# An attention turn of two score tiles and a whole PV step in place of three tiles and half steps

## The chip, the cores and the metric

The kernel runs on one core of one Trainium2 chip. The metric is device time in microseconds of one execution, the median of several runs. The core's engines are TensorE (PE in the profile, with its weight loads as PEld), VectorE (DVE), ScalarE (ACT), GpSimd (POOL) and SyncE (SP, which here issues DMAs).

## The reference

Two independent layers share a sequence of 2048 rows of 512 channels, and their outputs are laid side by side:

```python
q = (x @ wq).reshape(B, S, 32, 16).transpose(0, 2, 1, 3)   # 32 heads of 16
k = x @ wk                                                 # one key and value head
v = x @ wv
p = softmax(einsum("bhqd,bkd->bhqk", q, k) * 16 ** -0.5)
a = (p @ v).transpose(0, 2, 1, 3).reshape(B, S, 512) @ wo

k_shift = causal depthwise convolution of B_k, 4 taps
kv = k_shift * B_v
b = B_q * (long causal convolution of kv along S (by FFT) + kv * ssm_D)
out = concatenate([a, b], -1)
```

## The kernel before, in words

**Attention.** The 32 heads times 2048 queries are cut into 32 blocks (`NQ`) of 2048 rows: four heads with 512 queries each. For each block the kernel walks over the 16 key tiles of 128 (`NKT`), 512 steps in all. A step has two score tiles `s` of 128 keys by two heads of 512 queries (`scores`, L770 to L793): two fp16 matmuls of 512 columns at L784, on two row tiles of the array, and one exponential of 1024 columns on ACT at L792 that writes an fp32 tile `p`. `s` has three buffers of two PSUM banks each, `p` has seven. PV (`pv`, L795) multiplies `p` with the values, extended by a column of ones for the softmax's denominator, in fp32: four matmuls on four column tiles of the array, one for each head, that sum over the 16 key tiles in one PSUM bank `acc`. Here PV goes by half steps: at L821 each of the four matmuls has 256 columns, first the left half of a step, then the right. After 16 steps DVE copies the bank to `ao` (L831), SP sends it to DRAM (L833), and the next block takes the other bank of the pool `pf`, or the same one again.

The last block (`n == NQ - 1`) is cut by queries instead, in two halves of 256 columns (L806), so that the first half's result `al` (L815) is there early.

**The turn.** `attend` (L837) writes the order of the work by hand. A turn emits three score tiles (L841 to L844) and then the PV of up to three half steps. Three tiles of a turn fill all three buffers of `s`.

**Fill.** All else runs in the gaps: six generators (L1213) for the query projections, the convolution's transforms, its element-wise work on DVE, the output projection and so on. Each yields the cost of its next piece, in units for PE (four matmuls: 512 fp16 columns, or 128 fp32 columns) and nanoseconds for DVE, and `_Fill.step` (L1049) lets it go on when credit is left. `turn` (L1045) adds `RATE` to the credit once a turn, up to `MOST`. A generator that is neither the convolution's nor in a hurry gets at most `EASY` units a turn (L1065). `attend` calls `step` ahead of PV for a piece that continues an open PSUM bank, and behind PV for new ones (L857, L863); where a turn changes the PV bank (`full`, L854), the new ones come right ahead of the first PV of the new bank instead. Fill and PV share the two banks of `pf`: with `acc` in one, all fill groups pass through the other, and each has to be copied out by DVE before the next begins. Matmuls of the fill are at L203 (`mm`), transposes at L305, the bound at L638.

**The end.** In the last turn `fill.finish()` (L849) runs what is left of the fill; then come the PV of the last tiles and `last` (L988), which normalizes the second half of the last block on DVE (`over`, L975: six instructions with two 32x32 transposes), multiplies with the last rows of `wo` (`wl`), and adds the sums `wp` of all earlier heads. For row blocks 0 and 2 of the output `wp` is put into PSUM by a matmul with the identity and ACT copies the result; for 1 and 3 DVE adds it.

Of the kernel before, what the change touches and what calls it, by code (L numbers as in the profile page):

```python
# [8 lines left out]
F32 = mybir.dt.float32  # L9
# [5 lines left out]
ALU = mybir.AluOpType  # L15
# [4 lines left out]
P = 128  # L20
S = 2048
D = 512
H = 32
DH = 16
NKT = S // P
NQ = 4 * H // 4
# [19 lines left out]

RATE = 3.0, 2500.0
EASY = 2  # L50
MOST = 4.0, 2900.0
WO_AT = 240, 345, 430
OB = 5

# [36 lines left out]
WAIT = -1.0  # L91
# [4 lines left out]
class _Emit:  # L96
# [695 lines left out]
        self.nc.scalar.activation(p, s, AF.Exp, scale=DH**-0.5 / SC / SC)  # L792
        self.pt[u] = p  # L793

    def pv(self, x):  # L795


        nc, w = self.nc, self.w
        i, h = x // 2, x % 2
        n, k = i // NKT, i % NKT  # L800
        if n == NQ - 1:
            h, k = divmod(x % (2 * NKT), NKT)
            if k == 0:
                self.acc = self.bank()
            for j in range(4):
                nc.tensor.matmul(  # L806
                    self.acc[32 * j : 32 * j + 32, 0:256],
                    self.vx[:, k, :],
                    self.pt[x][:, j % 2, 256 * (j // 2) : 256 * (j // 2) + 256],
                    start=k == 0,  # L810
                    stop=k == NKT - 1,
                )
            if k == NKT - 1 and h == 0:
                self.al = w.tile([P, 512], F32, tag="r", bufs=1, name="al")
                nc.vector.tensor_copy(self.al[:, 0:256], self.acc[:, 0:256])  # L815
            return
        if k == h == 0:
            self.acc = self.bank()
        cols = slice(256 * h, 256 * h + 256)
        for j in range(4):  # L820
            nc.tensor.matmul(  # L821
                self.acc[32 * j : 32 * j + 32, cols],
                self.vx[:, k, :],
                self.pt[2 * i + j // 2][:, j % 2, cols],
                start=k == h == 0,
                stop=k == NKT - 1 and h == 1,
            )
        if k < NKT - 1 or h == 0:
            return
        a = w.tile([P, 512], F32, tag="ao", bufs=1, name=self.nm("ao"))  # L830
        nc.vector.tensor_copy(a, self.acc)  # L831
        if n < NQ - 2:
            nc.sync.dma_start(self.od[n], a)  # L833
        else:
            self.ao = a

    def attend(self, fill):  # L837
        self.od = self.dr.tile([NQ, P, 512], F32, name="od")
        x, steps = 0, NQ * NKT
        for u in range(3, 2 * steps + 3, 3):  # L840
            for t in range(u, min(u + 3, 2 * steps)):  # L841
                if t % 32 == 12 and 2 <= t // 32 + 1 < NQ:
                    self.stack(t // 32 + 1)
                self.scores(t)  # L844
            self.step = x // 2

            end = 2 * (min(u, 2 * steps) // 2) if u >= 2 * steps else min(x + 3, 2 * (u // 2))
            if u >= 2 * steps:
                fill.finish()  # L849
                self.lb = [self.wide()[:, 0, :] for _ in range(2)]  # L850
                self.mm(self.lb[0], self.ident, self.wp[0], stop=False)


            full = [y for y in range(x + 1, end) if y % (2 * NKT) == 0 or y == (2 * NQ - 1) * NKT]  # L854
            fill.turn()
            if not full:
                fill.step(self.step, False)  # L857
            for y in range(x, end):
                if y in full:
                    fill.step(self.step, True)  # L860
                self.pv(y)
            if not full:
                fill.step(self.step, True)  # L863
            x = end
        self.last()


    def heads(self, G):
# [53 lines left out]
    def wo_row(self, b, i, G, last):  # L922
        pairs = self.three(self.oc[G][:, :, i * P : (i + 1) * P], self.wo[G % 4])
        yield from self.products(b, pairs, last, 700 * last)

    def wo_part(self):
        nc, w, I = self.nc, self.w, self.I
        xr = self.out.rearrange("b (c p i) d -> (b c) p i d", c=4, p=P, i=4)
        for c in range(3):
            yield from self.after(("oc", 4 * c + 3))  # L930
            for i in range(4):
                b = yield from self.wo_rows(i, range(4 * c, 4 * c + 4))
                t = self.s2("wp", (512,))
                nc.vector.tensor_scalar(t, b, 1 / (OS * WS), None, ALU.mult)  # L934
                nc.sync.dma_start(xr[c][:, i, 0:D], t)
            self.seen.update(("wo", G) for G in range(4 * c, 4 * c + 4))

        yield from self.after(("oc", 13), f"q{3}")
        self.wp = [w.tile([P, D], F32, tag="wq", bufs=4, name=self.nm("wp")) for _ in range(4)]
        for i in range(4):  # L940
            b = yield from self.wo_rows(i, range(12, 14))
            nc.vector.tensor_scalar(self.wp[i], b, 1 / (OS * WS), None, ALU.mult)

        self.wl = []
        for q in range(2):
            t = w.tile([P, D], F32, tag="xt", bufs=2, name=self.nm("wl"))
            nc.gpsimd.memset(t, 0.0)
            for j in range(4):
                h = H - 8 + 4 * q + j
                nc.sync.dma_start(t[32 * j : 32 * j + DH, :], I["A_wo"][DH * h : DH * h + DH, :])  # L950
            self.wl.append(t)
        yield from self.after(("oc", 14))
        for i in range(4):
            b = []
            yield from self.wo_row(b, i, 14, True)
            nc.vector.scalar_tensor_tensor(self.wp[i], b[0], 1 / (OS * WS), self.wp[i], ALU.mult, ALU.add)
        both = w.tile([P, 2, 4, 512], F32, tag="in", bufs=1, name="lr")
        t, self.lr = both[:, 0], both[:, 1]
        while self.step < NKT * (NQ - 1) + 1:
            yield WAIT, 1  # L960
        for h in range(2):
            yield 0, 1800
            self.over(self.ao[:, 256 * h : 256 * h + 256], t, h)
        for i in range(4):
            if i == 2:

                while self.step < NKT * (NQ - 1) + NKT // 2 + 1:
                    yield WAIT, 1
                yield 0, 1800
                self.over(self.al[:, 0:256], self.lr, 0)  # L970
            b = []
            yield from self.columns(b, 0, t[:, 2, i * P : (i + 1) * P], self.wl[0], True, 700)
            nc.vector.tensor_tensor(self.wp[i], self.wp[i], b[0], ALU.add)

    def over(self, a, t, h):  # L975


        v = self.nc.vector
        r, s, o = (t[:, i, h * 256 : (h + 1) * 256] for i in range(3))
        v.transpose(r, a)  # L980
        col = r.rearrange("p (b c) -> p b c", c=32)[:, :, DH : DH + 1]
        v.tensor_scalar(col, col, 1e-30, None, ALU.max)
        v.reciprocal(col, col)
        v.tensor_copy(s.rearrange("p (b c) -> p b c", c=32), col.broadcast_to([P, 8, 32]))
        v.transpose(r, s)
        v.tensor_tensor(o, a, r, ALU.mult)

    def last(self):  # L988

        nc = self.nc  # L990
        xr = self.out.rearrange("b (c p i) d -> (b c) p i d", c=4, p=P, i=4)
        t = self.w.tile([P, 2, 4, 512], F32, tag="big", bufs=2, name="lb")[:, 0]
        s = self.lb + [self.wide()[:, 0, :], self.bank()]
        y = [self.s2("y", (512,)) for _ in range(4)]
        rows = lambda x, i: x[:, 2, i % 2 * P : (i % 2 + 1) * P]
        for i in range(2):
            self.mm(s[i], rows(self.lr, i), self.wl[1], start=i > 0)
        nc.scalar.copy(y[0], s[0])
        self.mm(s[2], self.ident, self.wp[2], stop=False)
        self.over(self.acc[:, 0:256], t, 0)  # L1000
        for i in range(2, 4):
            self.mm(s[i], rows(t, i), self.wl[1], start=i > 2)
        nc.vector.tensor_tensor(y[1], self.wp[1], s[1], ALU.add)
        nc.scalar.copy(y[2], s[2])
        nc.vector.tensor_tensor(y[3], self.wp[3], s[3], ALU.add)
        for i in range(4):
            (nc.scalar, nc.sync)[i % 2].dma_start(xr[3][:, i, 0:D], y[i])


class _Fill:  # L1010
# [34 lines left out]
    def turn(self):  # L1045
        self.used = 0
        self.credit = [min(c + r, m) for c, r, m in zip(self.credit, RATE, MOST)]

# [191 lines left out]
```

## Time and profile before

| | |
|---|---|
| time, median of 3 runs | 1048.03 us (1046.55 to 1048.33) |
| span of the profiled execution | 1043.5 us |
| median less span | 4.5 us |
| PE busy | 990.4 us (95%) |
| ACT busy | 972.4 us (93%) |
| DVE busy | 654.4 us (63%) |
| mean granted TensorE clock | 0.996 |

The span runs from the first to the last instruction of one profiled execution; the time of a run holds in addition what lies around that, so the two are 4.5 us apart here. In the views quoted below a row begins with its start in microseconds from the span's start, then its length, the engine, the source line, the operation, the tile written and the tiles read, and the number of instructions merged into the row; in square brackets stands the engine's idle time before it and what ended that. An fp32 matmul of the program shows as two records, so PV of three half steps, twelve matmuls, is x24.

### The profile page before, as it was taken

The page shows a single profiled execution, that of the slowest core. Times are in us where ns is not written, and L with a number is a line of the kernel's source. Part 1 is how long each engine was busy: PE and PEld are TensorE (multiplying, and loading weights), DVE is VectorE, ACT ScalarE, POOL GpSimd, SP SyncE. Part 2 cuts the span into 40 slices and gives each one's busy share as a digit, 9 for nine tenths or more (in the row PEclk, how much of TensorE's full clock was granted, in tenths as well). Part 3 has the DMA queues.
Part 4 walks back from the last instruction along what each step waited for, and adds up shares of the span by engine and source line. Part 5 has one row for each costly group of instructions (what it writes and reads, how often), then busy time and mean ns, then how long its engine had stood idle before and what let it go on. Part 6 is the DMA issues. An engine that isn't in the chain of part 4 may idle for free.

```text
span 1043.5 us, 31945 instructions
## 1 busy us (share of the span) xinstructions
PE 990.4 (95%) x14019; PEld 449.3 (43%) x14019; DVE 654.4 (63%) x881; ACT 972.4 (93%) x1039; POOL 105.0 (10%) x158
## 2 busy tenths in 40 slices
PE   6899999999999999999999999999999899999986
PEld 4344444444433334444444444444444334444432
DVE  4736873877497887776861578378888990211133
ACT  4699989999999999999999999999999999999994
POOL 4131301000000000030101312000000000121000
PEclk9999999999999999999999999999999999999999
DMA  7335524112211211031314534101032101331101
GB/s 243 128 97 181 190 77 167 45 51 82 91 56 45 75 35 40 22 122 57 96 56 132 183 123 149 42 20 44 33 97 71 52 29 40 109 121 45 51 2 44
DMA packets 47549, 87.30 MB, mean 84 GB/s; under 512 B 11132, under 2 KB 26026, under 8 KB 46380
## 3 DMA queue, kind: packets, MB, share of 16 engines
q1 hardware_dynamic: 33996, 43.50, 12.9%
q0 software_dynamic: 11648, 40.89, 12.1%
q8 instruction: 111, 1.82, 0.7%
q10 hardware_dynamic: 1760, 0.81, 0.3%
q14 instruction: 34, 0.28, 0.1%
HBM read 60.16 MB, written 25.02 MB: 82 GB/s over the span
## 4 chain that ended last, share of the span: by engine, by line
PE 70%; ACT 15%; DVE 8%; issue 6%; DMA 1%; ACTq 0%; SPq 0%
PE f L821 32%; PE s L784 22%; ACT p L792 14%; PE f L203 14%; DVE sp L141 2%; DVE ao L831 1%; PE f L305 1%; PE f L806 1%; DMA wqf<-in_A_wq 1%; DVE xT L540 1%; PE x L203 0%; ACT xT L539 0%; DVE sp L395 0%; DVE sp L255 0%; DVE t L362 0%
## 5 line engine op out<-in xcount | busy, mean ns | idle before, releaser
L792 ACT ACTIVATE p<-s 128x1024 f32<-128x1024 f32 x1024 | 960.1, 1037 | 41.5 <-PE s L784 35.9
L821 PE MATMUL f<-p,vx 128*32 128x256 f32 x7936 | 494.7, 381 | 8.1 <-DVE ao L831 8.1
L784 PE MATMUL s<-st,kst 49*128 49x512 f16 x2048 | 317.6, 380 | 19.1 <-ACT p L792 16.4
L821 PEld LDWEIGHTS f<-p,vx 128*32 128x32 f32 x7936 | 235.1, 110 | 196.9 <-issue 33.6
L784 PEld LDWEIGHTS <-kst 49*128 49x128 f16 x2048 | 100.1, 94 | 253.3 <-issue 206.5
L141 DVE TENSOR_TENSOR sp<-sp 128x1024 f32<-128x1024 f32 x96 | 111.5, 1213 | 0.0
L255 DVE COPY sp<-f 128x512 f32<-128x512 f32 x64 | 44.1, 689 | 63.6 <-PE f L203 62.5
L831 DVE COPY ao<-f 128x512 f32<-128x512 f32 x31 | 21.4, 691 | 71.4 <-PE f L821 71.4
L203 PE MATMUL f<-xT,wq 128*32 128x512 f16 x768 | 58.8, 391 | 0.1
L141 DVE TENSOR_TENSOR sp<-sp,sp 128x1024 f32<-128x1024 f32 x48 | 56.3, 1216 | 0.2
L203 PE MATMUL f<-wo,o 128*32 128x512 f16 x720 | 54.4, 383 | 0.0
L426 DVE TENSOR_TENSOR r<-f,q 128x512 f32<-128x512 f32 x16 | 11.0, 688 | 63.0 <-PE f L203 63.0
L259 POOL DMA_DIRECT2D ff<-in_ff x32 | 17.5, 548 | 266.7 <-PE f L203 266.7
L203 PE MATMUL f<-a,ff 128*32 128x256 f32 (+1 forms) x648 | 38.8, 338 | 1.6 <-DVE sp L255 1.6
L203 PE MATMUL f<-hT,ff 128*32 128x256 f32 (+1 forms) x648 | 38.8, 338 | 0.0
L203 PE MATMUL f<-sp,fi 128*32 128x256 f32 (+1 forms) x680 | 38.3, 331 | 0.0
L427 POOL DMA_DIRECT2D out<-r x16 | 11.5, 717 | 250.1 <-DVE rl L879 147.0
L364 DVE TENSOR_TENSOR a<-a,t 128x512 f32<-128x512 f32 x48 | 33.2, 691 | 1.5
L362 DVE TENSOR_TENSOR t<-kk,tpb 128x512 f32<-128x512 f32 x48 | 32.7, 681 | 0.0
L934 DVE TENSOR_SCALAR wp<-f 128x512 f32<-128x512 f32 x12 | 8.3, 690 | 38.8 <-PE f L203 38.8
L619 DVE TENSOR_SCALAR cut<-f 128x512 f32<-128x512 f32 x16 | 11.0, 689 | 32.3 <-PE f L203 32.2
L203 PEld LDWEIGHTS f<-a,ff 128*32 128x32 f32 x648 | 18.0, 109 | 17.2 <-issue 6.3
(141 smaller groups left out, 602.6 us busy)
## 6 DMA issues: line engine op xcount, KB each, us to landing
ff<-in_ff POOLq DMA_DIRECT2D x32, 256.0 KB, 5.0
od<-ao SPq DMA_DIRECT2D x30, 256.0 KB
kk<-in_B_k POOLq DMA_DIRECT2D x12, 640.0 KB, 4.9
qd<-qp SPq DMA_DIRECT2D x48, 128.0 KB
st<-qd SPq DMA_DIRECT2D x60, 98.0 KB
v<-in_B_v POOLq DMA_DIRECT2D x16, 256.0 KB, 4.8
hin<-in_B_ssm_k POOLq DMA_DIRECT2D x4, 1024.0 KB, 6.8
fi<-in_fi POOLq DMA_DIRECT2D x16, 256.0 KB, 3.8
```

The lines of the kernel that those rows point to most:

```text
L141: v.tensor_tensor(part(out), part(a), part(b), op)
L203: self.nc.tensor.matmul(out[j : j + 32], w[:, j : j + 32], x, start=start, stop=stop)
L255: self.nc.vector.tensor_copy(c[:, :, m, :], b[0].rearrange("p (q n) -> p q n", q=2))
L259: self.nc.gpsimd.dma_start(t, self.I[n][:, 2 * m2 : 2 * m2 + 2])
L362: nc.vector.tensor_tensor(t, kx(i), tap(i), ALU.mult)
L364: nc.vector.tensor_tensor(a, a, t, ALU.add)
L426: nc.vector.tensor_tensor(r, b[0].rearrange("p (i n) -> p i n", i=2), q[m2], ALU.mult)
L427: nc.gpsimd.dma_start(self.orr[:, 2 * m2 : 2 * m2 + 2, D + blk * CB : D + (blk + 1) * CB], r)
L784: self.nc.tensor.matmul(s[:, e, :], self.kst[rows, k * P : (k + 1) * P], part(rows), start=True, stop=True,)
L792: self.nc.scalar.activation(p, s, AF.Exp, scale=DH**-0.5 / SC / SC)
L821: nc.tensor.matmul(self.acc[32 * j : 32 * j + 32, cols], self.vx[:, k, :], self.pt[2 * i + j // 2][:, j % 2, cols], start=k == h == 0, sto ...
L831: nc.vector.tensor_copy(a, self.acc)
```

## The change

A turn of `attend` now emits two score tiles and then one whole step of PV: four matmuls of 512 columns (in the last block, two half steps as before). The bank of PV changes only between turns; there the fill's new pieces come ahead of PV. The credits are given per turn of two tiles: 1.8 units and 1700 ns, where a turn of three had 3.0 and 2500. `EASY` stays at 2 a turn.

At the end, the leftover fill runs before the PV of the last two tiles; the product for block 0 stands between these two, that for block 1 behind the second. DVE adds `wp` for blocks 0, 1 and 3, behind the normalization; ACT copies block 2 alone. SP's queue sends blocks 0 and 1, ACT's queue 2 and 3. In `wo_part`, the normalization of the first half of the last block moves behind the four products with `wl[0]`.

```diff
-RATE = 3.0, 2500.0
+RATE = 1.8, 1700.0
 EASY = 2
-MOST = 4.0, 2900.0
+MOST = 3.0, 2900.0
...
-    def pv(self, x):
+    def pv(self, i):
...
-        if k == h == 0:
+        if k == 0:
             self.acc = self.bank()
-        cols = slice(256 * h, 256 * h + 256)
         for j in range(4):
             nc.tensor.matmul(
-                self.acc[32 * j : 32 * j + 32, cols],
+                self.acc[32 * j : 32 * j + 32, :],
                 self.vx[:, k, :],
-                self.pt[2 * i + j // 2][:, j % 2, cols],
-                start=k == h == 0,
-                stop=k == NKT - 1 and h == 1,
+                self.pt[2 * i + j // 2][:, j % 2, :],
+                start=k == 0,
+                stop=k == NKT - 1,
             )
...
     def attend(self, fill):
         self.od = self.dr.tile([NQ, P, 512], F32, name="od")
-        x, steps = 0, NQ * NKT
-        for u in range(3, 2 * steps + 3, 3):
-            for t in range(u, min(u + 3, 2 * steps)):
+        steps = NQ * NKT
+        for i in range(steps - 1):
+            for t in range(2 * i + 3, min(2 * i + 5, 2 * steps)):
                 if t % 32 == 12 and 2 <= t // 32 + 1 < NQ:
                     self.stack(t // 32 + 1)
                 self.scores(t)
-            self.step = x // 2
...
+            self.step = i
             fill.turn()
-            if not full:
+            if i % NKT == 0 or i == (2 * NQ - 1) * NKT // 2:
+                fill.step(self.step, True)
+                self.pv(i)
+            else:
                 fill.step(self.step, False)
-            for y in range(x, end):
-                if y in full:
-                    fill.step(self.step, True)
-                self.pv(y)
-            if not full:
+                self.pv(i)
                 fill.step(self.step, True)
-            x = end
-        self.last()
+        self.last(fill)
...
-    def last(self):
+    def last(self, fill):
...
+        fill.finish()
         t = self.w.tile([P, 2, 4, 512], F32, tag="big", bufs=2, name="lb")[:, 0]
-        s = self.lb + [self.wide()[:, 0, :], self.bank()]
+        self.pv_last(4 * NQ * NKT // 2 - 2)
+        s = [self.wide()[:, 0, :]]
...
-        for i in range(2):
-            self.mm(s[i], rows(self.lr, i), self.wl[1], start=i > 0)
-        nc.scalar.copy(y[0], s[0])
+        self.mm(s[0], rows(self.lr, 0), self.wl[1])
+        self.pv_last(4 * NQ * NKT // 2 - 1)
+        self.over(self.acc[:, 0:256], t, 0)
+        s += [self.wide()[:, 0, :], self.wide()[:, 0, :], self.bank()]
+        self.mm(s[1], rows(self.lr, 1), self.wl[1])
         self.mm(s[2], self.ident, self.wp[2], stop=False)
-        self.over(self.acc[:, 0:256], t, 0)
         for i in range(2, 4):
             self.mm(s[i], rows(t, i), self.wl[1], start=i > 2)
-        nc.vector.tensor_tensor(y[1], self.wp[1], s[1], ALU.add)
+        for i in range(2):
+            nc.vector.tensor_tensor(y[i], self.wp[i], s[i], ALU.add)
         nc.scalar.copy(y[2], s[2])
         nc.vector.tensor_tensor(y[3], self.wp[3], s[3], ALU.add)
         for i in range(4):
-            (nc.scalar, nc.sync)[i % 2].dma_start(xr[3][:, i, 0:D], y[i])
+            (nc.sync, nc.scalar)[i // 2 % 2].dma_start(xr[3][:, i, 0:D], y[i])
```

More of the change, by code (lines that the diff above doesn't have):

```diff
@@ L793, in scores @@
         self.pt[u] = p
-    def pv(self, x):
+    def pv(self, i):
         nc, w = self.nc, self.w
-        i, h = x // 2, x % 2
         n, k = i // NKT, i % NKT
         if n == NQ - 1:
[L802 to L815, printed above, removed]
+            for x in (2 * i, 2 * i + 1):
+                self.pv_last(x)
             return
-        if k == h == 0:
+        if k == 0:
             self.acc = self.bank()
-        cols = slice(256 * h, 256 * h + 256)
         for j in range(4):
             nc.tensor.matmul(
-                self.acc[32 * j : 32 * j + 32, cols],
+                self.acc[32 * j : 32 * j + 32, :],
                 self.vx[:, k, :],
-                self.pt[2 * i + j // 2][:, j % 2, cols],
-                start=k == h == 0,
-                stop=k == NKT - 1 and h == 1,
+                self.pt[2 * i + j // 2][:, j % 2, :],
+                start=k == 0,
+                stop=k == NKT - 1,
             )
-        if k < NKT - 1 or h == 0:
+        if k < NKT - 1:
             return
@@ L835, in pv, with pv_last @@
             self.ao = a
+    def pv_last(self, x):
+        nc, w = self.nc, self.w
+        h, k = divmod(x % (2 * NKT), NKT)
+        if k == 0:
+            self.acc = self.bank()
+        for j in range(4):
+            nc.tensor.matmul(
+                self.acc[32 * j : 32 * j + 32, 0:256],
+                self.vx[:, k, :],
+                self.pt[x][:, j % 2, 256 * (j // 2) : 256 * (j // 2) + 256],
+                start=k == 0,
+                stop=k == NKT - 1,
+            )
+        if k == NKT - 1 and h == 0:
+            self.al = w.tile([P, 512], F32, tag="r", bufs=1, name="al")
+            nc.vector.tensor_copy(self.al[:, 0:256], self.acc[:, 0:256])
     def attend(self, fill):
         self.od = self.dr.tile([NQ, P, 512], F32, name="od")
-        x, steps = 0, NQ * NKT
-        for u in range(3, 2 * steps + 3, 3):
-            for t in range(u, min(u + 3, 2 * steps)):
+        steps = NQ * NKT
+        for i in range(steps - 1):
+            for t in range(2 * i + 3, min(2 * i + 5, 2 * steps)):
                 if t % 32 == 12 and 2 <= t // 32 + 1 < NQ:
@@ L844, in attend @@
                 self.scores(t)
-            self.step = x // 2
[L847 to L854, printed above, removed]
+            self.step = i
             fill.turn()
-            if not full:
+            if i % NKT == 0 or i == (2 * NQ - 1) * NKT // 2:
+                fill.step(self.step, True)
+                self.pv(i)
+            else:
                 fill.step(self.step, False)
-            for y in range(x, end):
-                if y in full:
-                    fill.step(self.step, True)
-                self.pv(y)
-            if not full:
+                self.pv(i)
                 fill.step(self.step, True)
-            x = end
-        self.last()
+        self.last(fill)
     def heads(self, G):
@@ L964, in wo_part @@
         for i in range(4):
[L965 to L970, printed above, removed]
             b = []
@@ L973, in wo_part @@
             nc.vector.tensor_tensor(self.wp[i], self.wp[i], b[0], ALU.add)
+        while self.step < NKT * (NQ - 1) + NKT // 2 + 1:
+            yield WAIT, 1
+        yield 0, 1800
+        self.over(self.al[:, 0:256], self.lr, 0)
     def over(self, a, t, h):
```

## The prediction, made before the changed kernel ran

> **What bounds the kernel now.** I read the page first: the engine sums, the chain that ended last, and the groups.
>
> ```profile
> span 1043.5 us, 31945 instructions
> PE 990.4 (95%) x14019; PEld 449.3 (43%) x14019; DVE 654.4 (63%) x881; ACT 972.4 (93%) x1039; POOL 105.0 (10%) x158
> ...
> PE 70%; ACT 15%; DVE 8%; issue 6%; DMA 1%; ACTq 0%; SPq 0%
> ...
> L792 ACT ACTIVATE p<-s 128x1024 f32<-128x1024 f32 x1024 | 960.1, 1037 | 41.5 <-PE s L784 35.9
> L821 PE MATMUL f<-p,vx 128*32 128x256 f32 x7936 | 494.7, 381 | 8.1 <-DVE ao L831 8.1
> ```
>
> Two engines are near full: ACT with 1024 exponentials, TensorE with scores, PV and the fill (projections, convolution, output matmuls). The chain runs through PE for 70%, so ACT mostly waits for PE and not the reverse. The next view, the timeline, tells what a turn costs on each. First a stretch with no fill:
>
> ```profile
> 805.29 17.52 ACT L792 ACTIVATE p<-s 128x1024 f32<-128x1024 f32 x19
> ...
> 818.60 1.50 PE L821 MATMUL f<-p,vx 128*32 128x256 f32 x24
> ...
> 821.03 0.39 PE L784 MATMUL s<-st,kst 49*128 49x512 f16 x2 [0.39 <-ACT p L792]
> ```
>
> Nineteen exponentials in 17.52 us: less the last one's own 1.04, that is 18 starts, **0.916 us a tile**, 2.75 us a turn of three. PE waits 0.39 us here for the score buffer of the third tile: ACT is the bound. Now a stretch where every turn carries three fill units (a unit is four matmuls, one row of tiles):
>
> ```profile
> 519.28 15.54 ACT L792 ACTIVATE p<-s 128x1024 f32<-128x1024 f32 x16
> ...
> 528.03 1.47 PE L821 MATMUL f<-p,vx 128*32 128x256 f32 x24
> 529.43 0.98 PE L784 MATMUL s<-st,kst 49*128 49x512 f16 x6
> 530.34 0.83 PE L203 MATMUL f<-wo,o 128*32 128x512 f16 x12
> 530.99 1.47 PE L821 MATMUL f<-p,vx 128*32 128x256 f32 x24
> 532.39 0.82 PE L784 MATMUL s<-st,kst 49*128 49x512 f16 x6
> 533.15 0.83 PE L203 MATMUL f<-wo,o 128*32 128x512 f16 x12
> 533.81 0.39 PE L821 MATMUL f<-p,vx 128*32 128x256 f32 x4
> ```
>
> Starts count, the ends are modelled. PV to scores is 1.40 us (530.99 to 532.39), scores to fill 0.76 (532.39 to 533.15), three units 0.66 (533.15 to 533.81), so a unit is 0.22. The turn is 2.82, the one before it 2.96 (528.03 to 530.99), because its scores took 0.91: the third tile had to wait for its buffer. Together 2.89, and ACT runs at (15.54 - 1.04) / 15 = 0.967 a tile. So a turn of n units costs PE 2.16 + 0.22 n, against 2.75 on ACT; up to two units fit, and three cost 2.89, because all three score buffers belong to one turn and nothing is left to even out a heavy turn.
>
> Where the 2.16 goes matters for the change. Six rounds of PV stream 6 x 0.216 = 1.29 and take 1.40; three score tiles stream 0.65 and take 0.76. **Each turn pays 0.11 us twice for changing between PV or fill and scores.**
>
> **The wide PV matmul.** The end of the trace has fp32 matmuls 512 wide and 256 wide (each fp32 matmul shows twice):
>
> ```profile
> 1030.91 1.05 PE L806 MATMUL f<-p,vx 128*32 128x256 f32 x16
> ...
> 1031.78 1.90 PE L203 MATMUL x<-wl,lr 128*32 128x512 f32 x16
> ...
> 1034.35 1.04 PE L203 MATMUL x<-wl,lb 128*32 128x512 f32 x8
> ```
>
> A second group of four 512-wide ones adds 1.90 - 1.04 = 0.86 us. Three groups of 256 take 1.50, two take 1.05: 0.43 each. So the wide form streams as long as two halves; its price is bounded by 0.86 a step from above and perhaps 0.01 less. I take 0.86: nothing is gained by it. The Trainium skill, "TensorEngine Tiling (Array Packing)", section Instruction Overhead, gives each matmul about 60 cycles of overhead. Read as an addition to the streaming it would make halves dearer than a whole; the 0.43 beside 0.86 leaves no room for that, so the trace decides against it (rival D).
>
> **The turn.** The order of both built programs gives the turns. Before: 340 turns, by units 0: 19, 1: 21, 2: 144, 3: 128, more: 28. After: 510 turns, 0: 64, 1: 99, 2: 326, 3: 20, more: 1. (Four 256-wide fill matmuls count as two units, four transposes as three.) The limit of two units for threads that are not in a hurry holds per turn, and a turn is now two tiles, so a turn of two units becomes the rule.
>
> PE, new: scores 0.76 - 0.22 = 0.54, PV 1.40 - 1.29 + 0.86 = 0.97, so 1.51 + 0.22 n. ACT: 2 x 0.916 = 1.83. No unit 1.51, one 1.73, two 1.95, three 2.17.
>
> - Before: 184 x 2.75 + 128 x 2.89 + 28 x 3.1 (four units 3.04, five 3.26) = 963.
> - After, PE alone: 64 x 1.51 + 99 x 1.73 + 326 x 1.95 + 20 x 2.17 + 2.4 = 949. ACT alone: 933. The dearer of the two turn by turn: 163 x 1.83 + 326 x 1.95 + 46 = 980.
>
> Which of 949 and 980 holds depends on slack. Now two of the three score buffers are filled in a turn, so one finished tile lies between PE and ACT: PE may be late by about 0.6 us (a tile of 0.916 less the score and its hand-over) before ACT stops, and light turns give it back. Four turns of two units mostly stand in a row, then one of one unit: 4 x 1.95 + 1.73 = 9.53 against 5 x 1.83 = 9.15, so in the dense stretches PE stays the bound at 0.953 a tile (0.963 before). Adding up the turns in the program's order, with 0.6 us of lateness forgiven, gives **965**.
>
> The extra switches are the price in this: 170 more turns x 0.22 = 37 us of PE work, which the looser coupling has to pay for. The Trainium skill, same page, section Key Properties, says that a change of tiling mode drains TensorE; with the drain of "TensorE: Matmul & The Clock Gate", Single matmul latency (398 cycles at 2.4 GHz, an estimate of 0.166 us), the switches would be 340 x 0.166 = 56 us and the sum up to 19 us dearer. The trace shows 0.11, and that decides.
>
> **What the sum leaves out**, measured on before:
>
> ```profile
> 33.32 1.94 ACT L792 ACTIVATE p<-s 128x1024 f32<-128x1024 f32 x2 [7.71 <-PE s L784]
> ...
> 1019.65 7.54 ACT L792 ACTIVATE p<-s 128x1024 f32<-128x1024 f32 x8
> ```
>
> The exponentials last from 33.3 to 1027.2, 994 us; the classes gave 963. Of the 31 left, part is the change of the PV bank every 16 steps:
>
> ```profile
> 505.99 0.85 PE L784 MATMUL s<-st,kst 49*128 49x512 f16 x6
> 506.77 0.64 PE L821 MATMUL f<-p,vx 128*32 128x256 f32 x8
> 507.23 0.83 PE L203 MATMUL f<-sp,fi 128*32 128x256 f32 x16
> 507.50 0.69 DVE L831 COPY ao<-f 128x512 f32<-128x512 f32 x1 [0.85 <-PE f L821]
> 508.25 1.07 PE L821 MATMUL f<-p,vx 128*32 128x256 f32 x16 [0.19 <-DVE ao L831]
> 509.25 0.82 PE L784 MATMUL s<-st,kst 49*128 49x512 f16 x6
> ```
>
> That turn took 3.26 (505.99 to 509.25), about 0.5 over its kind, since the next group of PV needs the bank that DVE empties 1.48 us after the old one's last four matmuls began. 31 changes x 0.5 = 16. After, a change always falls between two turns: the last step's 0.86, 0.11, scores 0.54 and, mostly, two units 0.44 lie over it, 1.95 against about 1.7 (the last round is now 0.43 long). I keep 0.1 each, 3 us. The other 15 us are PE behind a DVE that is busy; DVE's work is the same (1.7 us of it offered per two tiles, 2.5 per three before), so I keep 15, less 2 for the half bank at the end, whose copy no longer stands right behind both halves of the normalization.
>
> ```profile
> L141 DVE TENSOR_TENSOR sp<-sp 128x1024 f32<-128x1024 f32 x96 | 111.5, 1213 | 0.0
> L255 DVE COPY sp<-f 128x512 f32<-128x512 f32 x64 | 44.1, 689 | 63.6 <-PE f L203 62.5
> ```
>
> One cover shrinks: a fill group ended ahead of PV and its successor behind PV share one bank. PV lay between with 1.29 us, now with 0.86, and DVE needs about 1.0 from the end of the last round (1.48 less two rounds of 0.22, above). In the order 37 groups stand so: 37 x 0.15 = 6 us. The bounds are 0 (slack absorbs it) and 1.2 (a 1213 ns instruction ahead of the copy). DVE waits for PE before these copies for 62.5 us, so it is mostly early, and I stay near the low end.
>
> Attention: 965 + 3 + 13 + 6 = 987, 7 less than 994.
>
> **The end.**
>
> ```profile
> 1032.03 0.45 DVE L980 STREAM_TRANSPOSE lb<-f 128x256 f32<-128x256 f32 x1 [1.03 <-PE f L806]
> ...
> 1033.77 0.42 DVE L986 TENSOR_TENSOR lb<-f,lb 128x256 f32<-128x256 f32 x1
> ...
> 1036.32 0.69 DVE L1005 TENSOR_TENSOR y<-wp,f 128x512 f32<-128x512 f32 x1 [1.53 <-PE f L203]
> ```
>
> The last exponential ends at 1027.19, but PV of the last two tiles starts at 1030.91, behind the leftover fill, and the normalization at 1032.03. After, no fill is left there by the order, and PV of the last tile follows its exponential: normalization follows the start of that group by 0.7 (before: 1030.91 + 0.43 to 1032.03), so at about 1027.19 + 0.05 + 0.7 = 1027.9, 4.1 earlier. Behind it stands the same chain (2.2 us of DVE, two groups of 0.86, an addition). The two additions that moved onto DVE (2 x 0.69 = 1.4) run beside those two groups (1.7); without that cover they would cost 1.4. Two outputs now leave on each queue; SP has the first pair, early, and ACT has the second, behind its own copy of the third block, with nothing queued after it, so the last transfer is no later. **4 us less.**
>
> Sum: 1043.5 - 7 - 4 = 1032.5 of span. The shown runs have a median of 1048.0, 4.5 above the span; so 1037.
>
> **Rivals.**
> - B, slower: DVE's copies. A fill group behind PV, and PV after a bank change, wait for the copy with less in front of them. If a copy finds DVE in the middle of a convolution instruction, the 37 groups cost 0.55 and the 31 changes 0.4 each, 33 us for the 9 above, and ACT stalls with them: 1037 + 24 = 1061. It decides from 13 us more than the sum holds, 0.2 us for each of the 68. For it: 326 turns are already at 1.95 on PE, so in a dense stretch nothing makes up for a wait. Against it: the 62.5 us that DVE waits for PE.
> - C, better: the spare tile absorbs those DVE waits too, so 965 stands alone: 1043.5 - 29 - 4 + 4.5 = 1015. Against it: in dense stretches PE is late already.
> - D, the wide matmul really is cheaper: 0.05 us a step on 496 steps, 25 us: 1012. The end of the trace speaks against it.
>
> **How the numbers follow.** Forecast 0.46 (own range 1029 to 1046), B 0.36, C 0.14, D 0.04. A change under 0.2% (2 us) can't be told from none. Of the forecast 0.39 is faster, 0.05 the same, 0.02 slower; of B 0.02 is the same. Faster 0.57, same 0.07, slower 0.36. The range runs from 1017, short of C, to 1062, just past B.
>
> **What would show it.** In the profile after: a timeline with turns of 1.95 where two units stand and 1.83 where none do; PV to scores 0.97; score waits on ACT fewer; bank changes without the 0.5; the last normalization under 1 us behind the last exponential. Wrong if a switch costs other than 0.11, if wide PV is not 0.86, or if PE's waits for DVE copies grow beyond 20 us.

## The result, and the profile after

| | before | after |
|---|---|---|
| time, median (9 runs each) | 1047.17 us (1044.93 to 1048.71) | 1050.45 us (1049.98 to 1051.77) |
| ratio to before | | 1.0031 (1.0021 to 1.0040) |
| span of the profiled execution | 1043.5 us | 1049.1 us |
| first exponential starts | 33.3 us | 32.1 us |
| first to last exponential | 993.9 us | 1004.6 us |
| last exponential to the end | 16.3 us | 12.4 us |

The change makes the kernel **slower by 0.3%**, about 3.3 us. 1037 had been forecast. The profiled execution of after has a time of 1050.92 us, 1.8 above its span. By that the profiled one of before took some 1045.3 us and was a quick one among its runs: of the 4.5 us between its span and the median, only 1.8 lie around the span. So the spans differ by 5.6 where the medians differ by 3.3.

The page of after, engine sums, the chain and the two large groups:

```profile
span 1049.1 us, 24505 instructions
PE 1006.4 (96%) x10299; PEld 276.2 (26%) x10299; DVE 654.2 (62%) x882; ACT 981.3 (94%) x1038; POOL 104.9 (10%) x158
...
PE 82%; DVE 9%; ACT 5%; issue 3%; DMA 1%; SPq 0%; ACTq 0%; DVEq 0%
...
L792 ACT ACTIVATE p<-s 128x1024 f32<-128x1024 f32 x1024 | 969.5, 1057 | 41.8 <-PE s L784 36.6
L807 PE MATMUL f<-p,vx 128*32 128x512 f32 x3968 | 522.4, 600 | 4.4 <-DVE gm L651 2.7
```

The chain runs through PE for 82% (70% before) and through ACT for 5% (15%): ACT now hardly ever sets the pace. Half the PV matmuls are gone, but each is twice as wide, and PE's busy time is larger (1006.4 us for 990.4).

A dense stretch in the timeline of after, PE alone:

```profile
836.65 0.60 PE L784 MATMUL s<-st,kst 49*128 49x512 f16 x4
837.19 0.61 PE L203 MATMUL f<-wo,o 128*32 128x512 f16 x8
837.63 1.03 PE L807 MATMUL f<-p,vx 128*32 128x512 f32 x8
838.60 0.61 PE L784 MATMUL s<-st,kst 49*128 49x512 f16 x4
839.13 0.61 PE L203 MATMUL f<-wo,o 128*32 128x512 f16 x8
839.58 1.03 PE L807 MATMUL f<-p,vx 128*32 128x512 f32 x8
840.54 0.60 PE L784 MATMUL s<-st,kst 49*128 49x512 f16 x4
841.07 0.40 PE L203 MATMUL f<-wo,o 128*32 128x512 f16 x4
841.30 1.03 PE L807 MATMUL f<-p,vx 128*32 128x512 f32 x8
842.26 0.61 PE L784 MATMUL s<-st,kst 49*128 49x512 f16 x4
```

Two units: 838.60 - 836.65 = 1.95 and 840.54 - 838.60 = 1.94 us; one unit: 842.26 - 840.54 = 1.72. Scores 0.54 (836.65 to 837.19), PV with its change 0.97 (837.63 to 838.60). These are the prices that the prediction had worked out from before, and no matmul here waits for ACT. The rows also tell which changes cost. From scores to fill, both fp16 but on two row tiles and on four column tiles, there are 0.11 us over the streaming (0.54 for 0.43). From fp16 fill to fp32 PV, both on column tiles, one unit takes 0.23 (841.07 to 841.30) and two take 0.44, so that 0.02 at most are left for the change. It is the change of tiles that costs, not that of the type.

What was not in them is a turn like this one (timeline of after; in brackets the idle time before the row and what ended it):

```profile
499.46 0.38 PE L638 MATMUL f<-qa,wb 128*32 128x512 bf16 x1
...
500.20 0.69 DVE L882 TENSOR_TENSOR o<-of,r 128x512 f16<-128x512 f32 x1
500.31 1.07 PE L807 MATMUL f<-p,vx 128*32 128x512 f32 x8
500.92 0.69 DVE L882 TENSOR_TENSOR of<-of,r 128x512 f32<-128x512 f32 x1
501.64 0.69 DVE L882 TENSOR_TENSOR o<-of,o 128x512 f16<-128x512 f32 x1
502.25 0.67 DVE L640 TENSOR_SCALAR gn<-f 8x512 f16<-8x512 f32 x1
502.85 0.67 DVE L651 TENSOR_REDUCE gm<-f 16x1 f32<-16x512 f32 x1
...
503.57 0.62 PE L203 MATMUL f<-xT,wq 128*32 128x512 f16 x4 [2.19 <-DVE gm L651]
504.12 1.03 PE L784 MATMUL s<-st,kst 49*128 49x512 f16 x4
504.83 1.94 ACT L792 ACTIVATE p<-s 128x1024 f32<-128x1024 f32 x2 [2.52 <-PE s L784]
```

PE writes the bound (L638) into the one bank that the fill has. The bank is free only when DVE has read it twice (L640, L651), and in DVE's queue three instructions of the heads' normalization (L882) stand ahead of these reads. The next fill group, and with it all that PE has to do behind it, waits 2.19 us, and then ACT has stood for 2.52. The starts of all 510 turns can be compared with what a turn of their kind takes on PE when nothing holds it up (for a turn without fill, with the 1.83 us of two exponentials). In after 29 turns took at least 0.25 us more than their kind, 29 us in all; this count includes the turns behind a wait, in which ACT has to catch up.

The waits views show the same in sums (waiting engine and line, what it waited for, total us, times, longest). Before:

```profile
PEld f L821 <- DVE ao L831: 16.1, 19, 1.7
...
PE f L821 <- DVE ao L831: 8.1, 19, 1.2
...
PEld f L203 <- DVE sp L255: 4.2, 6, 2.1
```

After:

```profile
PEld f L203 <- DVE sp L255: 18.9, 18, 3.2
...
PEld L203 <- DVE gm L651: 10.7, 9, 3.1
...
PEld f L807 <- DVE ao L817: 3.5, 16, 0.3
...
PE f L807 <- DVE gm L651: 2.7, 1, 2.7
```

The wait for the copy of a finished PV bank is gone, as forecast (16.1 to 3.5, the longest 0.3); waits for the bank of the fill have come in its place. The last row is one of them: there the first PV of a new block waits for a bank that the bound still holds.

### The profile page after: what moved, and what is told of

Its sections match the earlier page's. It is cut to its first block, busy times and chain, and to the rows that moved or that the text cites. A ratio compares the mean times of both kernels' runs of the same rounds, so it can differ in the third digit from the quotient of the medians.

```text
span 1049.1 us, 24505 instructions
## 1 busy us (share of the span) xinstructions
PE 1006.4 (96%) x10299; PEld 276.2 (26%) x10299; DVE 654.2 (62%) x882; ACT 981.3 (94%) x1038; POOL 104.9 (10%) x158
## 4 chain that ended last, share of the span: by engine, by line
PE 82%; DVE 9%; ACT 5%; issue 3%; DMA 1%; SPq 0%; ACTq 0%; DVEq 0%
PE f L807 36%; PE s L784 24%; PE f L203 20%; ACT p L792 4%; PE f L830 1%; DVE sp L141 1%; PE f L305 1%; DVE sp L255 1%; DVE a L364 1%; DMA wqf<-in_A_wq 1%; DVE t L362 1%; DVE xT L540 1%; DVE gx L248 0%; DVE gm L651 0%; DVE gn L640 0%
## 5 line engine op out<-in xcount | busy, mean ns | idle before, releaser
L792 ACT ACTIVATE p<-s 128x1024 f32<-128x1024 f32 x1024 | 969.5, 1057 | 41.8 <-PE s L784 36.6
L807 PE MATMUL f<-p,vx 128*32 128x512 f32 x3968 | 522.4, 600 | 4.4 <-DVE gm L651 2.7
L784 PEld LDWEIGHTS <-kst 49*128 49x128 f16 x2048 | 63.9, 94 | 375.4 <-issue 371.5
L807 PEld LDWEIGHTS f<-p,vx 128*32 128x32 f32 x3968 | 106.2, 109 | 108.6 <-issue 64.6
L255 DVE COPY sp<-f 128x512 f32<-128x512 f32 x64 | 44.1, 690 | 92.0 <-PE f L203 91.9
L203 PE MATMUL f<-wo,o 128*32 128x512 f16 x720 | 58.9, 385 | 0.4 <-DVE cut L619 0.4
L203 PE MATMUL f<-a,ff 128*32 128x128 f32 (+1 forms) x784 | 45.0, 316 | 4.3 <-DVE sp L255 4.3
L203 PE MATMUL f<-sp,fi 128*32 128x128 f32 (+1 forms) x792 | 43.6, 312 | 0.0
L203 PE MATMUL f<-hT,ff 128*32 128x256 f32 (+1 forms) x632 | 42.2, 346 | 0.0
L203 PEld LDWEIGHTS <-wq 128*32 128x32 f16 x768 | 14.2, 94 | 54.1 <-issue 41.2
L203 PEld LDWEIGHTS f<-sp,fi 128*32 128x32 f32 x792 | 17.9, 108 | 37.4 <-issue 31.0
```

Source lines behind the costliest of these rows:

```text
L203: self.nc.tensor.matmul(out[j : j + 32], w[:, j : j + 32], x, start=start, stop=stop)
L255: self.nc.vector.tensor_copy(c[:, :, m, :], b[0].rearrange("p (q n) -> p q n", q=2))
L784: self.nc.tensor.matmul(s[:, e, :], self.kst[rows, k * P : (k + 1) * P], part(rows), start=True, stop=True,)
L807: nc.tensor.matmul(self.acc[32 * j : 32 * j + 32, :], self.vx[:, k, :], self.pt[2 * i + j // 2][:, j % 2, :], start=k == 0, stop=k == NKT - 1,
```

## The experiments

All times are medians; the ratios are to before, measured beside each group of experiments (medians 1047.0, 1047.4 and 1048.1). The theory at the start: late copies on DVE ate the gain. The rival: the 170 more changes on PE did.

**1. The new end on the old turn.** `attend` of before; `last` and the order in `wo_part` of after.

```diff
             if u >= 2 * steps:
-                fill.finish()
-                self.lb = [self.wide()[:, 0, :] for _ in range(2)]
-                self.mm(self.lb[0], self.ident, self.wp[0], stop=False)
+                break
...
-        self.last()
+        self.last(fill)
```

> The turn of before (three tiles, half steps, its credits) with the end of after. The last exponential ends at 1027.2 of 1043.5 us before (16.3 us ahead of the end) and at 1036.7 of 1049.1 after (12.4). If the end is worth what the sum gave it, this kernel is 2 to 4 us faster than before (the leftover fill of four units still stands ahead of the last PV, which may keep up to 2 us). Rival: the 12.4 us are only possible because the fill is done by then; then nothing is gained, 0 us.

Measured 1049.49, ratio 1.0027 (1.0016 to 1.0038): not faster, slower. The timeline of its end:

```profile
1028.77 1.05 PE L203 MATMUL f<-wl,lr 128*32 128x256 f32 x16
...
1032.36 0.44 DVE L977 STREAM_TRANSPOSE lr<-al 128x256 f32<-128x256 f32 x1
...
1034.62 1.07 PE L203 MATMUL x<-wl,lr 128*32 128x512 f32 x8 [2.50 <-issue]
1035.47 0.64 PE L806 MATMUL f<-p,vx 128*32 128x256 f32 x8
...
1036.17 0.45 DVE L977 STREAM_TRANSPOSE lb<-f 128x256 f32<-128x256 f32 x1 [1.66 <-PE f L806]
```

Fill is still left at 1028.77, after the last exponential, and the normalization of the first half (1032.36), which now stands behind it, holds up the product at 1034.62 and so the last PV.

**2. The old end on the new turn.** `last` of before, the rest of after.

> After, with the end of before (the identity matmul for block 0, both last PV tiles together, ACT's copies for blocks 0 and 2). The new end on the old turn gained nothing. Theory now: the 3.9 us less between the last exponential and the end come from the fill being done, not from the order; then this is within 1 us of after (1050). Rival, as forecast: the order is worth them; then 1053 to 1055.

Measured 1050.93, ratio 1.0037 (1.0023 to 1.0051), against 1.0031 for after: the same, with 12.0 us behind the last exponential in its trace (12.4 in after, 18.4 in experiment 1). So the 3.9 us that after saves there do not come from the order of the end but from the fill being done by then.

**3. Half PV steps in the new turn.**

```diff
-        for j in range(4):
-            nc.tensor.matmul(self.acc[32 * j : 32 * j + 32, :], ...)
+        for h in range(2):
+            cols = slice(256 * h, 256 * h + 256)
+            for j in range(4):
+                nc.tensor.matmul(self.acc[32 * j : 32 * j + 32, cols], ...)
```

> After, with the PV step of a turn written as two halves of 256 columns, 8 matmuls for 4. If the wide matmul streams as long as two halves, the time is that of after within 2 us (ratio to before 1.001 to 1.005). Rival: wide matmuls save their issue; then this is 10 to 25 us slower than after (ratio 1.013 to 1.027).

Measured 1053.97, ratio 1.0068 (1.0055 to 1.0082), 3.5 us over after. That lies between the two expectations, near the first: if all of it is PV's, the wide matmul saves 3.5 / 496 = 7 ns a step. It is worth 0.3%, not 2%.

**4. Twice the changes.** Half of a PV step between the two score tiles:

```diff
                 self.scores(t)
+                if t % 2 and i % NKT and i // NKT < NQ - 1:
+                    self.pv_half(i, 0)
```

> After, with half of the PV step put between the two score tiles of a turn (fifteen steps of sixteen, all blocks but the last): the same matmuls in two halves, and four changes between PV and scores a turn for two, 465 turns. If a change costs 0.11 us of TensorE as read off the traces, that is 465 x 0.22 = 102 us more on the engine that bounds; some 10 us of it fall on light turns: 1130 to 1155. Rival: the 0.11 us is only how the trace models starts; then the time stays within 10 us of the half-step variant's 1054.

Measured 1166.18, ratio 1.1136 (1.1109 to 1.1163). Against the half steps of experiment 3, which have the same matmuls, that is 112 us for 465 turns, 0.24 us a turn, **0.12 us a change**. Its timeline, PE:

```profile
603.49 0.39 PE L784 MATMUL s<-st,kst 49*128 49x512 f16 x2
603.81 0.64 PE L822 MATMUL f<-p,vx 128*32 128x256 f32 x8
604.38 0.39 PE L784 MATMUL s<-st,kst 49*128 49x512 f16 x2
604.70 0.64 PE L822 MATMUL f<-p,vx 128*32 128x256 f32 x8
```

One score tile streams 0.22 us, as a fill unit does, and takes 0.32 (603.49 to 603.81); half a PV step streams 0.43 and takes 0.57 (603.81 to 604.38). The price of a change is real, and it is the one in the forecast: at 0.12 the 340 changes of the 170 more turns cost 41 us where the sum has 37, so the rival explains 4 us at most. The Trainium skill, "TensorEngine Tiling (Array Packing)", section Key Properties, states that changing the tiling mode drains TensorE. The runs agree in that each change costs, 0.12 us here.

**5 and 6. Without VectorE's part of the transforms.** In both kernels the instructions of `dft16` and of the spectral product are left out, and their credits are still spent, so that PE's order stays the same. The kernels leave out that part of the convolution.

```diff
-        yield 0, n
-        v.tensor_tensor(re(x1), re(x2), im(x3), add)
+        yield 0, n
```

After:

> After, without VectorE's instructions of the transforms and of the spectral product (their credits are still spent, so TensorE's order is the same). Theory: about 33 us in which TensorE waits for a busy VectorE ate the gain; they go, and the time falls by 22 to 30 us, to about 1025. Rival: TensorE's own work per turn (170 more changes at 0.22 us) is the cause; then the time falls by no more than the same cut does in the kernel before.

Before:

> Before, with the same cut of VectorE's instructions. Theory: here VectorE's lateness costs less, since score buffers, not TensorE, pace most turns, and the waits at the change of the PV bank stay: 8 to 14 us fall away, to about 1036, so that the new turn would be the faster one by about 10 us. Rival: as much falls away as in after, and the old turn stays ahead by some 3 us.

Measured 1044.89 (ratio 0.9982, 0.9973 to 0.9991) and 1043.28 (0.9968, 0.9956 to 0.9980): 5.6 us less in after, some 3.7 in before, where 22 to 30 and 8 to 14 were expected, though DVE's work is halved (329 and 328 us of 654). **The theory in this form falls**: VectorE's total load is the smaller part. Of the 29 us in long turns 19 are left, and the weight loads' wait for the copy L255 (here L202) is 18.3 us for 18.9. The timeline of after without that work has the same kind of wait:

```profile
750.47 0.38 PE L573 MATMUL f<-qa,wb 128*32 128x512 bf16 x1
750.72 0.69 DVE L752 COPY ao<-f 128x512 f32<-128x512 f32 x1 [1.46 <-PE f L742]
...
751.33 0.68 DVE L817 TENSOR_TENSOR o<-of,r 128x512 f16<-128x512 f32 x1
...
752.04 0.69 DVE L817 TENSOR_TENSOR of<-of,r 128x512 f32<-128x512 f32 x1
752.77 0.69 DVE L817 TENSOR_TENSOR o<-of,o 128x512 f16<-128x512 f32 x1
753.38 0.67 DVE L575 TENSOR_SCALAR gn<-f 8x512 f16<-8x512 f32 x1
...
753.98 0.67 DVE L586 TENSOR_REDUCE gm<-f 16x1 f32<-16x512 f32 x1
...
754.79 1.94 PE L742 MATMUL f<-p,vx 128*32 128x512 f32 x8 [2.71 <-DVE gm L586]
```

DVE was idle for 1.46 us just before (750.72), and yet PE waits 2.71, as long as at the same place in after: here it is the work given out at once in front of the reads that counts. The new turn is not the faster one even here.

**7 to 10. How much VectorE gets per turn.** That amount is a credit: 1700 ns a turn, saved up to 2900, in after. Each of these is after with one line changed. The pieces of the fill then fall on other turns; PE's own work in the 510 turns, counted by kind, stays at 954 us (952 with 1500).

```diff
-MOST = 3.0, 2900.0
+MOST = 3.0, 1900.0
```

> After, with VectorE's credit capped at 1900 ns instead of 2900. If bursts out of saved credit (1.6 turns' worth, 1.05 before) put work ahead of the copies that TensorE waits for, the 29 us of long waits shrink by 8 to 15 us: 1036 to 1043. Rival: the work ahead of the copies is given out by other threads at its fixed times; then it changes by less than 3 us.

Measured 1041.45, ratio 0.9946 (0.9932 to 0.9960): 9 us less than after.

```diff
-RATE = 1.8, 1700.0
+RATE = 1.8, 1550.0
```

> After, with 1550 ns of VectorE's work offered per turn for 1700, 775 ns a tile for 850 (833 before). If VectorE falls behind because light turns last only 1.73 to 1.83 us, the long waits shrink by 8 to 15 us: 1036 to 1043; a rival loss is that the transforms end some 60 us later and leave fill for the end, 3 to 6 us. If the waits come from single pieces of work in front of a copy, it changes by less than 3 us.

Measured 1038.55, ratio 0.9917 (0.9902 to 0.9932): 12 us less.

With 1600 in that place:

> After, with VectorE's credit cut by 6% to 1600 ns. Light turns last 1.73 to 1.83 us on TensorE and ACT, so 1700 leaves VectorE no room beside what the credits don't count, 1550 left some and gave 1038.6. Theory: most of that gain is here too, 1039 to 1044. If only single coincidences were moved, it lies anywhere between 1037 and 1052, above all not between its neighbours.

Measured 1036.15, ratio 0.9896 (0.9881 to 0.9911): 14 us less and more than the 1550 gave: outside the 1039 to 1044 expected, and not between its neighbours, which was the sign named for single coincidences. They move a result by 2 or 3 us at least.

With 1500:

> After, with 1500 ns. If the pace offered is what counts, long waits shrink a little more than at 1550, but eight units of fill are left behind for the end, some 2 to 4 us: 1037 to 1042.

Measured 1032.85, ratio 0.9857 (0.9842 to 0.9872): nearly 18 us less, again below what was expected. The leftover that was feared is there all the same:

```profile
1011.94 1.02 ACT L792 ACTIVATE p<-s 128x1024 f32<-128x1024 f32 x1 [0.19 <-PE s L784]
...
1014.30 1.07 PE L203 MATMUL f<-wl,lr 128*32 128x512 f32 x8 [0.81 <-DVE wp L960]
...
1018.30 1.06 PE L203 MATMUL x<-wl,lr 128*32 128x512 f32 x8 [2.50 <-issue]
```

Fill still runs at 1014.30, behind the last exponential, and 18.3 us lie between that and the end (12.4 in after), so it costs 6 us. First to last exponential is 980.1 us, 24 less than in after.

**11. Both.** 1550 a turn and 1900 at most.

> After, with 1550 ns a turn and the cap at 1900 ns as well. Alone they gave 1038.6 and 1041.5. If pace and bursts are two causes, both together give 1033 to 1037; if they are the same waits, 1037 to 1041.

Measured 1032.36, ratio **0.9847 (0.9834 to 0.9861)**, 18 us under after: level with the 1500, and it beats both kernels. Each of the five ways to give VectorE less at once gained 9 to 18 us. The page of this one:

```profile
span 1031.1 us, 24469 instructions
PE 999.3 (97%) x10283; PEld 277.0 (27%) x10283; DVE 655.7 (64%) x882; ACT 978.8 (95%) x1038; POOL 105.2 (10%) x158
...
PE 89%; ACT 5%; DVE 3%; issue 2%; DMA 1%; SPq 0%; ACTq 0%; DVEq 0%
...
L792 ACT ACTIVATE p<-s 128x1024 f32<-128x1024 f32 x1024 | 967.1, 1052 | 24.3 <-PE s L784 19.4
```

and its waits:

```profile
PEld f L203 <- DVE sp L255: 12.4, 15, 0.9
...
PEld L203 <- DVE gm L651: 5.8, 8, 0.7
```

DVE's work is the same 655 us, but its share of the chain falls from 9% to 3%, the longest waits of the fill from 3.2 and 3.1 us to 0.9 and 0.7, and ACT's wait for scores from 36.6 to 19.4. Of the 29 us in long turns 9 are left, in 15 turns. The same count follows the times of the others, 1600 against 1550 included: 22 us with the cap, 16 with 1550, 13.5 with 1600 and 5 with 1500, where the end takes 6 back. So what these cuts gain is the time of the long turns.

**12. The control: a cut of 5% in the old turn.**

```diff
-RATE = 3.0, 2500.0
+RATE = 3.0, 2380.0
```

> Before, with VectorE's credit cut to 2380 ns a turn (793 a tile for 833, 5% less); the fill left for the end is the same. Theory: a turn of three is at least 2.75 us long, so VectorE kept up with 2500 already, and the cut gains no more than 3 us: 1044 to 1048. Rival: late VectorE costs the old turn as much as the new one; then 5 to 8 us fall away here too, 1039 to 1042, and the new turn's gain is not its own.

Measured 1047.16, ratio 0.9997 (0.9988 to 1.0006): nothing, where 6% (the 1600) took 14 us off the new turn. By this cut the gain of experiments 7 to 11 belongs to the new turn; larger cuts and a lower cap were not tried in the old one, nor a rate above 1700 in the new one.

## Why the prediction was wrong, point by point

The sign was wrong; the range (1017 to 1062) held the time. Forecast were 1032.5 us of span, measured 1049.1: 16.6 us more. The time is off by 13 only because the 4.5 us added to the span were too much by 3, for the reason given with the result; that is luck.

- **Prices of a turn: right.** 1.95, 1.73 and 1.51 were forecast; after has 1.94 to 1.97, 1.72 to 1.75 and, in a turn without fill that nothing holds up, 1.53. Counted by kind, the 510 turns hold 954 us of PE's own work for the 949.
- **The price of a change: right**, 0.11 forecast, 0.12 measured by experiment 4. The 0.166 us estimated from the Trainium skill, "TensorE: Matmul & The Clock Gate", section Single matmul latency, is too dear: the measured price decides.
- **Wide PV: right.** 0.86 a step; 7 ns of saving, where up to 10 were left open. Rival D is out.
- **Slack of one score buffer: right.** The 61 turns without fill that have wide PV last 105.7 us, where 61 x 1.53 = 93.3 are PE's own: 12 us are lost on light turns, and 16 had been left for it (965 less 949).
- **The change of the PV bank: right.** 31 x 0.4 = 12 us were to be saved; the weight loads' wait for that copy fell from 16.1 to 3.5 us. Two changes stand out in after, 1.7 and 3.0 us over their kind (at 410.8 and 757.9 us): PV there waits for a bank of the fill, 1.64 and 2.71 us, which belongs to the step that failed.
- **The end: right.** 3.9 us less behind the last exponential, 4.1 forecast, and the sum put them down to no fill being left there. Experiments 1 and 2 bear that out: the new order of the end by itself is worth nothing. One sign was missed by little: the last normalization begins 1.1 us behind the last exponential, not under 1, since the product for block 0 stands ahead of the last PV.
- **DVE's lateness: this step failed.** "The other 15 us are PE behind a DVE that is busy; DVE's work is the same (1.7 us of it offered per two tiles, 2.5 per three before), so I keep 15". With 3 for the bank changes, 6 for the shorter cover and 2 taken off, 22 us were set down. Of the 1003 us from the first turn's start to the last one's, 954 are PE's own and 12 are light turns; 37 remain, 15 more than the 22, and 29 of the 37 lie in the 29 long turns. Adding the 5 us of turn prices and taking off the 4 of light turns, that is the miss of attention: 1003 for 987 (from the first exponential to the last it is 1004.6). That the 15 us in before are waits for DVE stood on no row; with half of DVE's work gone experiment 6 was 3.7 us faster.

Why the step failed: the amount offered per tile was compared and found about equal, and the waits were held constant for that. But what a late copy costs is not equal. In after PE sets the pace, and a copy has one PV step of 0.97 us ahead of the next use of its bank where it had 1.40. Giving VectorE 5% less per turn gains nothing in the old turn (experiment 12), while each of the cuts in the new one gains 9 to 18 us (7 to 11). That the old turn's waits for its score buffers covered such copies is my reading of it, and was not tried. That the price lies more in what is ahead of the copy at that moment than in the load is what experiment 5 shows: with half of DVE's work left out, 19 of the 29 us remain. Rival B named the mechanism, put the condition at "in the middle of a convolution instruction", and gave it 0.36 and 24 us: the 15 us are about two thirds of that size. What stood in front was not only the convolution: the waits of 2.71, 2.19 and 1.64 us had the normalization of the heads ahead of the copy or of the bound's reads, most of the others instructions of the convolution.

Open is how the 5.6 and the 3.7 us of experiments 5 and 6 come about, and why 1600 beats 1550; both are near what moves from one coincidence to another.

## What to carry to other kernels

Where two engines are near full and one is made the bound on purpose, do not carry over the old waits on a third engine as a constant: here 22 us were kept for them and 37 came. When the length of a turn changes, the amount of work handed to an in-order engine per turn and its saved maximum have to be set anew and tried on their own; here those two numbers were worth 18 us, more than five times the effect of the whole change. And a gain at the end of a kernel should be tried alone: this one came from the fill being done, and not from the new order.

## What the runs showed of the hardware

A change between fp32 matmuls on four column tiles and fp16 matmuls on two row tiles costs TensorE 0.12 us (112 us for 930 changes); one from fp16 to fp32 on the same column tiles 0.02 at most (0.23 us for one fill unit and 0.44 for two). Four fp32 matmuls of 512 columns are only 7 ns quicker than eight of 256. An exponential of 1024 columns starts every 0.916 us when nothing holds it up, though each lasts 1.04.
